# The recurrence's h held on chip by channel, and the chosen tokens' columns copied at register offsets

## The chip, the core and the metric

One core of a Trainium2 chip runs the whole kernel in one launch. The metric is the device time of one execution in microseconds, the median of several runs. The engines that work here are PE (TensorE, matmuls and transposes), DVE (VectorE), ACT (ScalarE), POOL (GpSimd) and SP (SyncE, which only issues DMAs). ACT and POOL issue some DMAs too.

## What is computed

```python
# x, f_logit: (4, 5056, 256); lower_bound: (256,)
f = lower_bound + (1 - lower_bound) * sigmoid(f_logit)
for t in range(5056):                  # for each of 4 batches and 256 channels
    h = f[:, t] * h + (1 - f[:, t]) * x[:, t]
    y[:, t] = h
tokens = y.reshape(20224, 256)
logits = tokens @ w_gate               # 8 experts
expert, gate = argmax(logits), softmax(logits) at the argmax
out = zeros(20224, 256)
for e in range(8):
    tok = the at most 80 tokens of expert e with the largest gate
    out[tok] = gate[tok] * (relu(tokens[tok] @ w1[e]) @ w2[e])   # w1 (8,256,1024), w2 (8,1024,256)
```

All is float32. At most 640 of the 20224 rows of the result are not zero.

## The kernel before, in words

The work has three stages.

**Stage 1, recurrence and logits (lines 105 to 283).** The sequence is cut into 10 groups of 512 tokens (the last one overlaps the one ahead of it), times 4 batches: 40 units of 512 tokens by 256 channels, run as a software pipeline in which each turn n of the loop at L271 does one step for several units. `load` (L126) brings f_logit and x of a unit, 512 KB each, token by partition. `gate` (L135, ACT) makes s, the complement of the sigmoid; `enter` (L139, POOL) makes u = s * x. `to_channels` (L143, PE) transposes both so that channels lie on the partitions: 8 transposes into `sp`, 8 into `up`, each half a unit in one PSUM bank, two buffers each. `decay` (L152, ACT) makes the factor a from sp, and `scan` (L159, DVE) runs the recurrence along the free axis into a tile `h`, from the last column of the same batch one group earlier. h is then used twice. `to_tokens` (L167) transposes it back: 8 transposes into the one PSUM buffer `hp` in two halves, the first copied out by ACT and the second by DVE into `ht`, which SP writes to `h_dram` (512 KB a unit). `logits` (L192, PE) multiplies h by the gate weights. After every fourth unit (a group) `by_token` transposes the logits and `choice` (DVE) finds each token's expert. After 5 groups, and after the last, `gates` computes the gate values and `candidates` puts them into `cand`, a table of 128 rows (expert, batch, token modulo 4) by 1264.

**Stage 2, selection (L306 to L374).** The weights of all 8 experts (2 MB each) and the zeros for the whole result (20.7 MB) are issued on SP's queue ahead of it, in the order at L298 to L304. `largest` (L315, DVE) takes the 80 largest of each row of `cand` in 10 rounds; they go through DRAM (`val_dram`, `id_dram`, issued by ACT) into 8 rows of 1280, and `largest` runs again. From the places found, 8 indirect DMAs (POOL, L362) fetch the token numbers of each expert's 80 slots, and 8 more (L368) fetch the tokens' rows of h from `h_dram`, 80 by 256.

**Stage 3, experts (L376 to L411).** `hidden(e)` transposes the rows (2 PE transposes), scales them (`xt`, DVE), and does 32 matmuls (order counts 16, each issued as two) with w1 and a ReLU (ACT). `result(e)` does the matmuls with w2, scales by the gate value (`y`, DVE) and scatters 80 rows (POOL). `hidden(e + 1)` stands ahead of `result(e)`.

The order of each engine's instructions is the order in which the program is written (`tc.manual_schedule`); waits between engines are semaphores that the tile layer puts in. An engine runs its own instructions in order.

Of the kernel before, what the change touches and what calls it, by code (L numbers as in the profile page):

```python
# [16 lines left out]
P = 128  # L17
# [5 lines left out]
def kernel(  # L23
# [46 lines left out]
    h_dram = dram.tile([N, D], F32, name="h_dram")  # L70
# [29 lines left out]
    shift = consts.tile([P, n_grp, C, E], F32, name="shift")  # L100
    chosen = consts.tile([P, n_grp, C, E], F32, name="chosen")
    nc.gpsimd.memset(shift, 0.0)
    ctx.enter_context(tc.manual_schedule())

    with tc.tile_pool(name="ld", bufs=5) as ld, \
         tc.tile_pool(name="sup", bufs=3) as sup, \
         tc.tile_pool(name="apool", bufs=2) as apool, \
         tc.tile_pool(name="hpool", bufs=B + 4) as hpool, \
         tc.tile_pool(name="htok", bufs=3) as htok, \
         tc.tile_pool(name="gsm", bufs=2) as gsm, \  # L110
         tc.tile_pool(name="psu", bufs=2, space=PSUM) as psu, \
         tc.tile_pool(name="ptp", bufs=1, space=PSUM) as ptp, \
         tc.tile_pool(name="plg", bufs=1, space=PSUM) as plg:

        xs, fs, sts, uts, sps, ups, decays, hs, lgs, lts, gms = ({} for _ in range(11))

        def setup():
            nc.vector.tensor_scalar(omlb, lb, -1.0, 1.0, ALU.mult, ALU.add)
            nc.vector.tensor_scalar(nomlb, lb, 1.0, -1.0, ALU.mult, ALU.add)
            for o in range(DC):  # L120
                nc.vector.tensor_scalar_mul(wg[:, o], wg[:, o], omlb[:, ds(o, 1)])
            bp = plg.tile([P, 1], F32, name="bp", tag="ct")
            nc.tensor.transpose(bp, base_row, ident[:1, :1])
            nc.vector.tensor_copy(base, bp)
# [10 lines left out]
        def gate(n):  # L135
            sts[n] = sup.tile([P, R, D], F32, name="s_t", tag="s_t")
            nc.scalar.activation(sts[n], fs.pop(n), ACT.Sigmoid, scale=-1.0)  # L137

        def enter(n):  # L139
            uts[n] = sup.tile([P, R, D], F32, name="u_t", tag="u_t")  # L140
            nc.gpsimd.tensor_tensor(uts[n], sts[n], xs.pop(n), ALU.mult)  # L141

        def to_channels(n, src, dst, tag):  # L143
            for o in range(DC):
                ps = psu.tile([P, G], F32, name=tag, tag=tag)
# [6 lines left out]
        def decay(n):  # L152
            for o in range(DC):
                a = apool.tile([P, G], F32, name="a", tag=f"a{o}")
                nc.scalar.activation(a, sps.pop((n, o)), ACT.Identity,  # L155
                                     scale=nomlb[:, ds(o, 1)], bias=1.0)
                decays[n, o] = a

        def scan(n):  # L159
            hs[n] = hpool.tile([P, DC, G], F32, name="h", tag="h")  # L160
            for o in range(DC):
                nc.vector.tensor_tensor_scan(  # L162
                    hs[n][:, o], decays.pop((n, o)), ups.pop((n, o)),
                    hs[n - B][:, o, ds(used(n // B - 1) - 1, 1)] if n >= B else 0.0,
                    ALU.mult, ALU.add)

        def to_tokens(n):  # L167
            g, b = divmod(n, B)
            ht = htok.tile([P, R, D], F32, name="ht", tag="ht")
            half = R // 2  # L170
            for i in range(2):
                hp = ptp.tile([P, half, D], F32, name="hp", tag="hp")
                for r in range(half):
                    for o in range(DC):
                        nc.tensor.transpose(hp[:, r, ds(o * P, P)],  # L175
                                            hs[n][:, o, ds((i * half + r) * P, P)], ident)
                copy = nc.scalar.copy if i == 0 else nc.vector.tensor_copy
                copy(ht[:, ds(i * half, half)], hp)  # L178
            lap = G - used(g)
            skip = lap if g == n_grp - 2 else 0  # L180
            out_t = h_dram[ds(b * S + first(g), G)].rearrange("(r p) d -> p r d", p=P)
            if skip:
                whole = (G - skip) // P
                nc.sync.dma_start(out=out_t[:, :whole], in_=ht[:, :whole])
                part = G - skip - whole * P
                if part:
                    nc.sync.dma_start(out=out_t[:part, whole], in_=ht[:part, whole])
            else:
                nc.sync.dma_start(out=out_t, in_=ht)


        def logits(n):  # L192
# [3 lines left out]
            hv = hs[n].rearrange("c o (p r) -> c o p r", r=R)  # L196
# [14 lines left out]
        def choice(g):  # L211
# [4 lines left out]
            def small(shape, name):  # L216
# [4 lines left out]
            sh = shift[:n_p, g]  # L221
# [5 lines left out]
            rv = small([C], "rv")  # L227
            nc.vector.tensor_reduce(rv, eq, AX.X, ALU.max)
            nc.vector.tensor_tensor(chosen[:n_p, g], eq,
                                    rv.unsqueeze(2).broadcast_to(full), ALU.is_equal)  # L230


        def gates(g0, g1):
            n = g1 - g0
            sh = shift[:, ds(g0, n)]
# [6 lines left out]
            for g in range(g0, g1):  # L242
                n_p = rows(g)
                gm = gsm.tile([P, E, C], F32, name="gm", tag="gm")[:n_p]
                nc.vector.tensor_tensor(
                    gm.rearrange("p e c -> p c e"), chosen[:n_p, g],
                    gt[:n_p, g - g0].unsqueeze(2).broadcast_to([n_p, C, E]), ALU.mult)
# [21 lines left out]
        AHEAD = 4  # L269
# [173 lines left out]
```

## Time and profile before

| | us |
|---|---|
| median of 3 runs | 488.58 (488.48 to 489.03) |
| the profiled execution, its own time | 486.84 |
| its span, first to last instruction | 485.1 |
| PE busy | 270.0 (56%) |
| DVE busy | 251.3 (52%) |
| ACT busy | 131.7 (27%) |
| POOL busy | 123.3 (25%) |
| moved by DMA | 101.93 MB |

The busy shares are means over three stages that have little in common, so they say little. Slices of the span show it: PE works in the first 58% and in the last 17% of the span and stands still between, while DVE is nearly full there. So the page is read stage by stage: which engine has work all the time, what the others wait for, and what the waiting costs in that stretch.

### The profile page before, as it was taken

The numbers are of one execution on the slowest core, as the hardware profiler recorded it, in microseconds if no ns is written. First come the engines' busy times: TensorE is split into PE (matmuls) and PEld (weight loads), VectorE is DVE, ScalarE is ACT, GpSimd is POOL, SyncE is SP. The second block draws the span as 40 slices with busy tenths as digits, with TensorE's granted clock in tenths as the row PEclk, the third lists the DMA queues.
The fourth block names the chain that finished last, engine by engine and source line by source line (L and its number), as shares of the span: only waits on it lengthen the run. The fifth ranks groups of instructions, "written<-read, shape, count | busy, mean of one in ns | idle before, by whom it ended". The sixth has DMA issues, their size and how long they took to land. (4 is left out here: it accounts for less than half of the span.)

```text
span 485.1 us, 5330 instructions
## 1 busy us (share of the span) xinstructions
PE 270.0 (56%) x2053; PEld 198.1 (41%) x2053; DVE 251.3 (52%) x335; ACT 131.7 (27%) x192; POOL 123.3 (25%) x77
## 2 busy tenths in 40 slices
PE   4886768768686486867687720000000003998985
PEld 3654545545554254545464410000000003977773
DVE  1555564555654755555644569995299951001010
ACT  4643443535254343435444120000000000101110
POOL 5543333414331132423331011000000037101011
PEclk9999897989798598989979865555555555599999
DMA  8988695969586456877852219999999501000000
GB/s 278 340 288 265 204 292 168 287 186 293 171 274 210 130 181 211 269 252 224 280 171 86 88 53 371 427 432 433 420 402 400 208 0 35 20 7 15 7 15 14
DMA packets 77001, 101.93 MB, mean 210 GB/s; under 512 B 3752, under 2 KB 73384, under 8 KB 75696
## 3 DMA queue, kind: packets, MB, share of 16 engines
q1 hardware_dynamic: 75104, 100.15, 59.5%
q0 software_dynamic: 1024, 1.31, 1.0%
q8 instruction: 16, 0.26, 0.2%
q10 hardware_dynamic: 848, 0.13, 0.2%
q14 instruction: 9, 0.07, 0.0%
HBM read 59.43 MB, written 42.16 MB: 209 GB/s over the span
## 5 line engine op out<-in xcount | busy, mean ns | idle before, releaser
L141 POOL TENSOR_TENSOR u_t<-s_t,x_t 128x1024 f32<-128x1024 f32 x40 | 94.7, 2368 | 162.4 <-ACT s_t L137 157.4
L162 DVE TENSOR_TENSOR_SCAN h<-a,h,up 128x512 f32<-128x512 f32 x72 | 87.9, 1263 | 0.0
L178 DVE COPY ht<-hp 128x512 f32<-128x512 f32 x40 | 27.7, 692 | 107.4 <-PE hp L175 107.4
L147 PE MATMUL up<-ident,u_t 128*128 128x128 f32 x320 | 56.6, 307 | 40.3 <-DVE h L162 39.0
L175 PE MATMUL hp<-ident,h 128*128 128x128 f32 x320 | 57.0, 306 | 27.1 <-ACT ht L178 27.1
L155 ACT ACTIVATE a<-sp,nomlb 128x512 f32<-128x512 f32 x80 | 51.1, 684 | 63.0 <-PE sp L147 61.5
L147 PEld LDWEIGHTS up<-ident,u_t 128*128 128x128 f32 x320 | 38.3, 154 | 57.2 <-issue 32.0
L348 PE MATMUL slots<-ident,at2f 8*80 8x8 f32 x1 | 0.2, 228 | 104.8 <-DVE at2f L344 104.8
L393 ACT ACTIVATE hid<-h_ps 128x480 f32<-128x480 f32 (+1 forms) x16 | 7.0, 438 | 184.7 <-PE h_ps L390 184.7
L175 PEld LDWEIGHTS hp<-ident,h 128*128 128x128 f32 x320 | 40.3, 155 | 38.6 <-ACT ht L178 37.8
L147 PE MATMUL sp<-ident,s_t 128*128 128x128 f32 x320 | 47.6, 297 | 4.2 <-ACT s_t L137 4.2
L178 ACT COPY ht<-hp 128x512 f32<-128x512 f32 x40 | 23.5, 586 | 85.5 <-PE hp L175 85.5
L147 PEld LDWEIGHTS sp<-ident,s_t 128*128 128x128 f32 x320 | 38.9, 152 | 15.9 <-issue 11.6
L199 PE MATMUL lg<-h,wg 128*32 128x128 f32 x640 | 44.1, 406 | 0.0
L137 ACT ACTIVATE s_t<-f_t 128x1024 f32<-128x1024 f32 x40 | 42.5, 1063 | 4.5 <-DMA f_t<-in_f_logit_dram 4.5
L348 PEld LDWEIGHTS slots<-ident,at2f 8*80 8x80 f32 x1 | 0.1, 138 | 105.1 <-DVE at2f L344 105.1
L390 PE MATMUL h_ps<-xt,w_sb 128*128 128x80 f32 x256 | 36.8, 313 | 5.0 <-issue 4.1
L390 PEld LDWEIGHTS h_ps<-xt,w_sb 128*128 128x128 f32 x256 | 35.7, 227 | 6.2 <-issue 4.9
L318 DVE MAX8 val<-cand 128x8 f32<-128x1264 f32 (+1 forms) x20 | 29.6, 1480 | 14.3 <-DMA cand<-val_dram 13.7
L402 DVE TENSOR_SCALAR y<-y_ps,gsl 80x256 f32<-80x256 f32 x8 | 3.8, 480 | 58.1 <-PE y_ps L399 58.1
L399 PE MATMUL y_ps<-w_sb,hid 128*80 128x256 f32 x128 | 30.6, 396 | 0.0
L319 DVE FIND_INDEX8 at<-val,cand 128x8 uint32<-128x1264 f32 (+1 forms) x20 | 29.4, 1470 | 0.0
(58 smaller groups left out, 181.1 us busy)
## 6 DMA issues: line engine op xcount, KB each, us to landing
f_t<-in_f_logit_dram SPq DMA_DIRECT2D x40, 512.0 KB, 5.0
x_t<-in_x_dram SPq DMA_DIRECT2D x40, 512.0 KB, 5.6
h_dram<-ht SPq DMA_DIRECT2D x36, 512.0 KB, 3.3
out_dram<-zero SPq DMA_DIRECT2D x9, 2048.0 KB, 24.3
w_sb<-in_moe_w_dram SPq DMA_DIRECT2D x16, 1024.0 KB, 11.6
out_dram<-zero SPq DMA_DIRECT2D x1, 1792.0 KB, 24.5
h_dram<-ht SPq DMA_DIRECT2D x4, 384.0 KB, 2.5
h_dram<-ht SPq DMA_DIRECT2D x4, 64.0 KB, 2.2
```

Source lines behind the costliest of these rows:

```text
L137: nc.scalar.activation(sts[n], fs.pop(n), ACT.Sigmoid, scale=-1.0)
L141: nc.gpsimd.tensor_tensor(uts[n], sts[n], xs.pop(n), ALU.mult)
L147: nc.tensor.transpose(ps[:, ds(r * P, P)], src[n][:, r, ds(o * P, P)], ident)
L155: nc.scalar.activation(a, sps.pop((n, o)), ACT.Identity, scale=nomlb[:, ds(o, 1)], bias=1.0)
L162: nc.vector.tensor_tensor_scan(hs[n][:, o], decays.pop((n, o)), ups.pop((n, o)), hs[n - B][:, o, ds(used(n // B - 1) - 1, 1)] if n >= B el ...
L175: nc.tensor.transpose(hp[:, r, ds(o * P, P)], hs[n][:, o, ds((i * half + r) * P, P)], ident)
L178: copy(ht[:, ds(i * half, half)], hp)
L199: nc.tensor.matmul(lgs[g][ds(r * LC, LC), b], wg[:, o], hv[:, o, :, r], start=o == 0, stop=o == DC - 1, skip_group_check=True)
L318: nc.vector.max(out=top, in_=src)
L319: nc.vector.max_index(out=at[:, ds(k, TOP)], in_max=top, in_values=src)
L390: nc.tensor.matmul(h_ps[:, c], w1_sb[e][:, o, ds((c0 + c) * P, P)], xt[:, o], start=o == 0, stop=o == DC - 1, skip_group_check=True)
L399: nc.tensor.matmul(y_ps, hid[:, c], w2_sb[e][:, c], start=c == 0, stop=c == FC - 1)
```

## The change

h is no longer written to DRAM. One tile `h_all` holds it for all 20224 tokens, channel by partition (128 partitions of 2 x 20224 floats, 158 KB each). `decay` writes the factor straight into h's place, and `scan` runs in place there. `to_tokens`, the `ht` copies and the writes to `h_dram` are gone. To make room, `gate` and `enter` work in place in the loaded tiles (4 buffers of each, where there were 5 and 3 of the products), and loads are issued 3 turns ahead where it was 4; `up` has 4 PSUM buffers where it had 2. `chosen` is not stored: `choice` keeps only the winning code (`pick`), and `gates` makes the one-hot table again, one DVE instruction more for each group.

Only expert 0's weights are loaded ahead of the selection; the zeros follow in 40 writes of at most 512 KB. After the token numbers have come (one tile `tok` of 80 by 8 now), they are cast, transposed to `trow` (8 rows of 80) and loaded into registers, 16 at a time. For each of the 640 slots one engine then copies one column of `h_all` (128 partitions, 2 elements) into `xe`, at the offset in the register. Runs of 16 slots go to DVE, ACT, POOL, DVE, ACT for each expert. Then `h_all` is released, and the weights of experts 1 to 7 are loaded into its room. `hidden` scales `xe` with no transpose.

The core of the diff (the parts left out are names and pools):

```diff
-    h_dram = dram.tile([N, D], F32, name="h_dram")
...
+    h_all = hpool.tile([P, DC, N], F32, name="h_all")
...
         def gate(n):
-            sts[n] = sup.tile([P, R, D], F32, name="s_t", tag="s_t")
-            nc.scalar.activation(sts[n], fs.pop(n), ACT.Sigmoid, scale=-1.0)
+            sts[n] = fs.pop(n)
+            nc.scalar.activation(sts[n], sts[n], ACT.Sigmoid, scale=-1.0)
...
         def decay(n):
             for o in range(DC):
-                a = apool.tile([P, G], F32, name="a", tag=f"a{o}")
-                nc.scalar.activation(a, sps.pop((n, o)), ACT.Identity,
+                nc.scalar.activation(h_all[:, o, ds(spot(n), G)], sps.pop((n, o)), ACT.Identity,
                                      scale=nomlb[:, ds(o, 1)], bias=1.0)
...
+                h = h_all[:, o, ds(spot(n), G)]
                 nc.vector.tensor_tensor_scan(
...
+                    h, h, ups.pop((n, o)),
+                    h_all[:, o, ds(spot(n) - 1, 1)] if n >= B else 0.0, ALU.mult, ALU.add)
-        def to_tokens(n):
...
-                nc.sync.dma_start(out=out_t, in_=ht)
...
+                nc.vector.tensor_tensor(oh, revexp[:n_p].unsqueeze(1).broadcast_to(full),
+                                        pick[:n_p, g].unsqueeze(2).broadcast_to(full),
+                                        ALU.is_equal)
...
-        AHEAD = 4
+        AHEAD = 3
...
-            unit(to_tokens, n - 1)
...
+    EARLY = 1
...
+    for e in range(EARLY):
+        weights(wpool, e)
...
+    ZR = 4
...
-            nc.gpsimd.indirect_dma_start(
-                out=xe, out_offset=None, in_=h_dram,
-                in_offset=bass.IndirectOffsetOnAxis(ap=toks[e], axis=0))
...
+        rp = psl.tile([E, K], F32, name="rp")
+        nc.tensor.transpose(rp, tokf, ident[:K, :K])
+        trow = xpool.tile([E, K], I32, name="trow")
+        nc.vector.tensor_copy(trow, rp)
...
+        SHARE = 16
+        X = []
+        for e in range(E):
+            xe = xpool.tile([P, DC, K], F32, name=f"xe{e}")
+            for i, k in enumerate(range(0, K, SHARE)):
+                engine, copy = ways[i % len(ways)]
+                n = min(SHARE, K - k)
+                _, at_tok = nc.values_load_multi_w_load_instructions(
+                    trow[ds(e, 1), ds(k, n)], engines=(engine,), min_val=0, max_val=N - 1,
+                    skip_runtime_bounds_check_because="token numbers come from iota")
+                for j, v in enumerate(at_tok):
+                    copy(xe[:, :, ds(k + j, 1)], h_all[:, :, ds(v, 1)])
+            X.append(xe)
+        hpool.release()
+        wlate = ctx.enter_context(tc.tile_pool(name="wlate", bufs=1, side="right"))
+        for e in range(EARLY, E):
+            weights(wlate, e)
...
-            for o in range(DC):
-                nc.tensor.transpose(xt_ps[:, o], X[e][:, ds(o * P, P)], ident[:K, :K])
...
-                nc.vector.tensor_scalar_mul(xt[:, o], xt_ps[:, o], omlb[:, ds(o, 1)])
+                nc.vector.tensor_scalar_mul(xt[:, o], X[e][:, o], omlb[:, ds(o, 1)])
```

PE in stage 1, before, around the end of a group (`sp` and `up` are the transposes of s and u, `hp` those of h, `lg` the logits, `lt` their transposes):

```order
L147 MATMUL sp<-ident,s_t 128x128 x8
L147 MATMUL up<-ident,u_t 128x128 x8
L175 MATMUL hp<-ident,h 128x128 x8
L199 MATMUL lg<-h,wg 32x128 x8
L207 MATMUL lt<-ident,ls 128x128 x4
```

The same place with the change:

```order
L152 MATMUL sp<-ident,f_t 128x128 x8
L152 MATMUL up<-ident,x_t 128x128 x8
L177 MATMUL lg<-h_all,wg 32x128 x8
L185 MATMUL lt<-ident,ls 128x128 x4
L152 MATMUL sp<-ident,f_t 128x128 x8
```

The eight `hp` transposes between `up` and `lg` are gone; nothing else moved on PE.

DVE between selection and experts, with the change (`goal` is the row to scatter to, `trow` the token numbers by expert; ISA is a register instruction that works out the copy's address from a token number):

```order
L352 TENSOR_TENSOR goal_2034<-tok,far 80x1
L359 CAST trow<-rp 8x80
L371 TENSOR_LOAD trow
L375 ISA
L375 COPY xe_2040<-h_all 128x2
```

The last two rows stand there 16 times behind each of 16 such loads, 256 copies in all; ACT has the same 16 and 256, POOL 8 and 128. Before, DVE went from the eighth `goal` straight to the `xt` scaling.

SP, before, behind the last write of h (the two DMAs of expert 1 and those of experts 2 to 7 follow in the same form):

```order
L189 DMA h_dram<-ht 128x4x256 x4
L295 DMA w_sb_2640<-in_moe_w_dram 128x2x1024
L296 DMA w_sb_2648<-in_moe_w_dram 128x8x256
L295 DMA w_sb_2641<-in_moe_w_dram 128x2x1024
L296 DMA w_sb_2649<-in_moe_w_dram 128x8x256
L302 DMA out_dram<-zero 128x4096 x9
```

SP with the change, behind the last load of x:

```order
L274 DMA w_sb_1863<-in_moe_w_dram 128x2x1024
L276 DMA w_sb_1865<-in_moe_w_dram 128x8x256
L290 DMA out_dram<-zero 128x1024 x39
L290 DMA out_dram<-zero 128x512
L274 DMA w_sb_4012<-in_moe_w_dram 128x2x1024
```

Of the weights only expert 0's stand ahead of the zeros; the row that starts with w_sb_4012 (expert 1) waits for the last copy on DVE, ACT and POOL.

## Rows read from the trace of the kernel before

**Rows 1.** Busy time by stretch: us, PE, PEld, DVE, ACT, POOL busy (instructions), PEclk, DMA share, GB/s.
```profile
4.00:15.00 11.00, 7.61 (x40) 7.06 (x40) 4.14 (x8) 6.94 (x9) 7.14 (x3) 1.00 1.08 376
...
289.46:394.71 105.25, 0.30 (x2) 0.21 (x2) 89.12 (x101) 0.00 (x0) 3.92 (x3) 0.50 0.89 358
...
408.25:485.10 76.85, 67.30 (x398) 56.70 (x398) 7.01 (x23) 7.00 (x16) 11.89 (x13) 0.88 0.06 16
```
**Rows 2.** Waits between 20 and 260 us: total us, times, longest.
```profile
PE up L147 <- DVE h L162: 35.5, 37, 2.8
...
PE hp L175 <- ACT ht L178: 23.7, 35, 0.7
```
**Rows 3.** Timeline of a unit in stage 1: start us, us, instruction [idle before].
```profile
103.89 2.37 POOL L141 TENSOR_TENSOR u_t<-s_t,x_t 128x1024 f32<-128x1024 f32 x1 [6.84 <-ACT s_t L137]
...
109.07 1.10 PE L199 MATMUL lg<-h,wg 128*32 128x128 f32 x16
...
109.47 2.37 POOL L141 TENSOR_TENSOR u_t<-s_t,x_t 128x1024 f32<-128x1024 f32 x1 [3.20 <-ACT s_t L137]
109.79 2.44 DVE L162 TENSOR_TENSOR_SCAN h<-a,h,up 128x512 f32<-128x512 f32 x2
...
110.10 1.09 PE L147 MATMUL sp<-ident,s_t 128*128 128x128 f32 x8
...
110.79 1.26 ACT L155 ACTIVATE a<-sp,nomlb 128x512 f32<-128x512 f32 x2 [1.40 <-PE sp L147]
...
111.20 0.63 PE L147 MATMUL up<-ident,u_t 128*128 128x128 f32 x4
```
**Rows 4.** Timeline, the first unit's transposes of u.
```profile
9.36 1.97 PE L147 MATMUL up<-ident,u_t 128*128 128x128 f32 x8 [1.12 <-POOL u_t L141]
```
**Rows 5.** Timeline of POOL around the gate values of the first five groups.
```profile
160.58 2.34 POOL L141 TENSOR_TENSOR u_t<-s_t,x_t 128x1024 f32<-128x1024 f32 x1 [10.30 <-ACT s_t L137]
172.91 2.37 POOL L141 TENSOR_TENSOR u_t<-s_t,x_t 128x1024 f32<-128x1024 f32 x1 [9.99 <-ACT s_t L137]
```
**Rows 6.** Timeline, end of stage 1.
```profile
268.61 0.66 PE L147 MATMUL up<-ident,u_t 128*128 128x128 f32 x4 [0.45 <-DVE h L162]
...
280.16 0.29 DVE L220 TENSOR_REDUCE mx<-lt 128x16 f32<-128x128 f32 x1 [1.71 <-PE lt L207]
...
289.46 1.48 DVE L318 MAX8 val<-cand 128x8 f32<-128x1264 f32 x1
```
**Rows 7.** Groups by line and form: xcount | busy us, mean ns | idle before.
```profile
L318 DVE MAX8 val<-cand 8x8 f32<-8x1280 f32 x10 | 14.8, 1482 | 14.0 <-DMA cand<-val_dram 13.7
...
L393 ACT ACTIVATE hid<-h_ps 128x480 f32<-128x480 f32 x8 | 4.6, 571 | 180.9 <-PE h_ps L390 180.9
...
L393 ACT ACTIVATE hid<-h_ps 128x160 f32<-128x160 f32 x8 | 2.4, 304 | 3.8 <-PE h_ps L390 3.8
```
**Rows 8.** DMA issues: count, KB each, us to landing.
```profile
tok<-id_dram,place POOLq DMA_INDIRECT x8, 2.2
...
val_dram<-val ACTq DMA_DIRECT2D x1, 40.0 KB, 9.3
```
**Rows 9.** Timeline from the selection to the first expert.
```profile
394.25 0.16 DVE L351 CAST place<-slots 80x8 int32<-80x8 f32 x1 [0.39 <-PE slots L349]
394.33 0.15 DVE L353 COPY gsl<-slots 80x8 f32<-80x8 f32 x1
...
403.40 0.91 POOL L362 DMA_INDIRECT tok<-id_dram,place  x1 [0.30 <-issue]
...
408.26 7.12 PE L390 MATMUL h_ps<-xt,w_sb 128*128 128x80 f32 x32 [0.40 <-DVE xt L382]
```
**Rows 10.** Instructions of L403: count, duration ns min/median/max, first and last start.
```profile
L403 POOLq MOVE  x8: 29/29/29, 405.8 to 477.2; - x8
```
**Rows 11.** Timeline between two experts in stage 3.
```profile
436.44 0.48 DVE L402 TENSOR_SCALAR y<-y_ps,gsl 80x256 f32<-80x256 f32 x1 [7.16 <-PE y_ps L399]
436.84 0.50 DVE L382 TENSOR_SCALAR xt<-xt_ps,omlb 128x80 f32<-128x80 f32 x2
...
437.23 2.99 PE L390 MATMUL h_ps<-xt,w_sb 128*128 128x80 f32 x25 [0.69 <-issue]
```

More of the change, by code (lines that the diff above doesn't have):

```diff
@@ L99, with spot @@
     BATCHES = 2
-    shift = consts.tile([P, n_grp, C, E], F32, name="shift")
-    chosen = consts.tile([P, n_grp, C, E], F32, name="chosen")
+    per_batch = -(-n_grp // BATCHES)
+    shift = consts.tile([P, per_batch, C, E], F32, name="shift")
     nc.gpsimd.memset(shift, 0.0)
+    pick = consts.tile([P, n_grp, C], F32, name="pick")
+    hpool = tc.alloc_tile_pool(name="hpool", bufs=1, side="right")
+    h_all = hpool.tile([P, DC, N], F32, name="h_all")
     ctx.enter_context(tc.manual_schedule())
[L105 to L112, printed above, removed]
+    with tc.tile_pool(name="ld", bufs=4) as ld, \
+         tc.tile_pool(name="gsm", bufs=1) as gsm, \
+         tc.tile_pool(name="pss", bufs=2, space=PSUM) as pss, \
+         tc.tile_pool(name="psu", bufs=4, space=PSUM) as psu, \
          tc.tile_pool(name="plg", bufs=1, space=PSUM) as plg:
-        xs, fs, sts, uts, sps, ups, decays, hs, lgs, lts, gms = ({} for _ in range(11))
+        xs, fs, sts, uts, sps, ups, lgs, lts, gms = ({} for _ in range(9))
+        def spot(n):
+            g, b = divmod(n, B)
+            return b * S + first(g)
         def setup():
@@ L226, in choice @@
                 op0=ALU.is_ge, op1=ALU.mult)
[L227 to L230, printed above, removed]
+            nc.vector.tensor_reduce(pick[:n_p, g], eq, AX.X, ALU.max)
         def gates(g0, g1):
             n = g1 - g0
-            sh = shift[:, ds(g0, n)]
+            sh = shift[:, ds(0, n)]
             nc.scalar.activation(sh, sh, ACT.Exp)
@@ L268, with begin @@
         batches = {g: (ends[i - 1] + 1 if i else 0, g + 1) for i, g in enumerate(ends)}
-        AHEAD = 4
+        AHEAD = 3
+        def begin(g):
+            return next(g0 for g0, g1 in batches.values() if g0 <= g < g1)
         setup()
@@ L302 @@
         nc.sync.dma_start(out=out_z[:, ds(k * D, n)], in_=zero[:, :n])
-    for e in range(2, E):
-        load_weights(e)
     with tc.tile_pool(name="sel", bufs=1) as sel, \
-         tc.tile_pool(name="xp", bufs=E) as xp, \
-         tc.tile_pool(name="mp", bufs=2) as mp, \
          tc.tile_pool(name="psl", bufs=1, space=PSUM) as psl, \
-         tc.tile_pool(name="psx", bufs=2, space=PSUM) as psx, \
          tc.tile_pool(name="psh", bufs=2, space=PSUM) as psh, \
@@ L366 @@
+        nc.vector.tensor_copy(tokf, tok)
+        goals = []
         for e in range(E):
-            xe = xp.tile([K, D], F32, name="xe", tag="xe")
-            nc.gpsimd.indirect_dma_start(
-                out=xe, out_offset=None, in_=h_dram,
-                in_offset=bass.IndirectOffsetOnAxis(ap=toks[e], axis=0))
-            X.append(xe)
-            goal = sel.tile([K, 1], I32, name=f"goal{e}")
-            nc.vector.tensor_tensor(goal, toks[e], far[:, ds(e, 1)], ALU.add)
-            goals.append(goal)
+            goal = sel.tile([K, 1], I32, name=f"goal{e}")
+            nc.vector.tensor_tensor(goal, tok[:, ds(e, 1)], far[:, ds(e, 1)], ALU.add)
+            goals.append(goal)
@@ new lines @@
+        rp = psl.tile([E, K], F32, name="rp")
+        nc.tensor.transpose(rp, tokf, ident[:K, :K])
+        trow = xpool.tile([E, K], I32, name="trow")
+        nc.vector.tensor_copy(trow, rp)
+        ways = [(mybir.EngineType.DVE, nc.vector.tensor_copy),
+                (mybir.EngineType.Activation, nc.scalar.copy),
+                (mybir.EngineType.Pool, nc.gpsimd.tensor_copy)]
+        SHARE = 16
[10 more added lines that the diff above has]
+                    copy(xe[:, :, ds(k + j, 1)], h_all[:, :, ds(v, 1)])
+            X.append(xe)
@@ L376, in hidden @@
+        hpool.release()
+        wlate = ctx.enter_context(tc.tile_pool(name="wlate", bufs=1, side="right"))
+        for e in range(EARLY, E):
+            weights(wlate, e)
+        mp = ctx.enter_context(tc.tile_pool(name="mp", bufs=2, side="right"))
         def hidden(e):
[L377 to L379 removed]
             xt = mp.tile([P, DC, K], F32, name="xt", tag="xt")
```

80 lines of the change are left out of this document (27 added, 53 removed).

## The prediction, made before the changed kernel had run

> **What bounds the kernel now.** I read the stretches first, then the waits inside the longest one, then one unit of it, then the two seams. The stretches [rows 1] show three stages: up to 289.5 us the recurrence, then 105 us in which DVE has 89 us of work and PE none, then 77 us in which PE has 67. The change touches the first stage, the seam between the second and the third, and what DMA moves meanwhile. In the first stage no engine is full. PE waits 35.5 us for scans to free an `up` buffer and 23.7 us for ACT to empty the one `hp` buffer [rows 2]. One unit shows the same [rows 3]: `u_t` starts every 5.58 us (103.89 and 109.47), while in it PE's own work without `hp` is short: 1.10 us from the start of the 8 `sp` transposes to the start of `up`, as much again for `up`, and 1.03 us for the logits (109.07 to 110.10), 3.23 us in all. DVE's two scans take 2.44 us, POOL 2.37, ACT's two factors 1.26. So a unit is 5.58 us long because of a loop (PE to ACT to PE through `hp`, PE to DVE to PE through `up`), and the end of each group adds to it: the wait ahead of `u_t` is 6.84 us there and 3.20 otherwise.
>
> **Stage 1.** Removed: 320 `hp` transposes, 80 copies, 40 writes of 512 KB. With them goes the first loop. The second has twice the buffers. What is late next? PE at 3.23 us a unit plus a quarter of the group's `lt` transposes, say 3.33; DMA, which with loads alone moved 376 GB/s at a full share in the first 15 us [rows 1], so 1.05 MB of a unit in 2.8 us; then DVE with 2.44 and its choice operations, POOL with 2.37. All are below the 5.58 of today, and PE is the longest. The loop through the load buffers is no longer than that: from the end of `up` in a buffer to the next `up` in it there are an issue, a landing and POOL's 2.37 us, for four units. I take 3.6 us a unit, the PE figure and a little for the engines missing each other. The bounds are 3.3 (PE alone) and the 5.58 of today. From the first unit's `up`, which ends at 11.3 us [rows 4] as before, 39 units at 3.6 give 140.4: 151.7 us. The gate values of the first five groups hold PE up in the middle: the two waits there are 10.30 and 9.99 us [rows 5] where a group's seam and a usual turn have 6.84 and 3.20 [rows 3], 10.2 us more. I keep that whole, 162 us; the five one-hot tables made again go into it. At the end the last `up` is at 269.3 us now and the first operation on the last logits at 280.2, 10.9 us [rows 6], most of it three units' `hp` work in turn; scan, logits, copy and transposes alone I put at 5.5. From there to the selection it is 9.3 us, plus five one-hot operations at 0.29 us (the price of `mx`), 10.7. So the selection starts at 178 us, not at 289.5: **minus 111 us**.
>
> **Selection.** Its DVE work is unchanged. Its one wait is 13.7 us for the 40 KB that go through DRAM [rows 7], of which 9.3 are the landing of `val` behind the zeros [rows 8]. The zeros now start with the last `up`, 16 us ahead of the selection, behind one expert's weights and not two: 22.8 MB at 358 GB/s and a share of 0.89 [rows 1], so 402 at a full share, take 57 us and end about 41 us into the selection. `val` leaves after 29 operations of 1.48 us [rows 6], 43 us into it. Two hops of the 2.2 us that a small transfer takes [rows 8] and their issues make 5 us: **minus 8.7**. If I am wrong about the queue, nothing is gained there; nothing is lost either, since the last zeros wait for `val`.
>
> **The seam, and the copies.** Token numbers come as before, the last issued at 403.4 us [rows 9], landed at 405.6. Now all eight must be there: cast, eight `goal` operations, a transpose and the cast to `trow`, 1.4 us. Then the copies, C; then the scaling, 0.6; the first expert's matmuls stood at 408.26 [rows 9], so **minus 0.7 plus C**. Nothing covers C: DVE scales expert 0's columns only behind its own 256 copies, so PE waits for all of them.
>
> C is the one term that the trace does not show. DVE and ACT carry 256 copies each, with a register instruction ahead of each and 16 loads of 16 registers; POOL has half. *Per copy:* the lower bound is 0.08 us, the distance of two small DVE operations (394.25 and 394.33 [rows 9]). For ACT the ReLUs of 480 and of 160 elements take 571 and 304 ns [rows 7], 0.83 ns an element, so 0.17 us without any element. The upper bound is that plus the 0.30 us that POOL's issue leaves between two DMAs at register-like work [rows 9], 0.47. A register move on POOL takes 29 ns [rows 10], far nearer to nothing than to 0.30, so address work should run ahead of the engine; I take 0.17 on ACT, the slower of the two: 256 x 0.17 = 43.5 us. *Per load of 16 registers:* the lower bound is 16 moves of 29 ns, 0.46 us; the upper 16 times 0.30, 4.8 us. It is a round trip to memory for a few words, so I take the row that is nearest to that, the 2.2 us of `tok` [rows 8]: 16 x 2.2 = 35 us. **C = 79 us**, between 28 (0.08 and 0.46) and 197 (0.47 and 4.8).
>
> The ReLUs read PSUM; the copies read SBUF, for which no row of ACT is small enough. [...]
>
> **Weights.** 14.7 MB wait for the last copy and then take 36 us at 402 GB/s. Expert 1's first MB is there after 2.6 us and a 2.2 us trip, 4.8 us; PE needs it after expert 0's 7.12 us [rows 9]. Each further expert needs 5.2 us of DMA and eight take PE 77 us [rows 1], so I cost this at nothing; its cover is PE's own work, and at half the rate the last experts would wait some 10 us. The transposes of `xe` go, but PE still stands between experts until DVE has done `y` and `xt` behind it (436.44 to 437.23 [rows 11]): nothing gained.
>
> **Sum.** 485.1 - 111 - 8.7 - 0.7 + 79 = 443.7 us of span. The profiled execution took 486.84, 1.7 more than its span, and the median of the runs, 488.58, is 1.7 more again: **447 us**, 41 less than now.
>
> **Rivals.**
> *Cheap columns.* Register work is hidden and loads are fast: C = 28, 396 us. For it: the 29 ns move; against it: no load of many values is that quick in this trace.
> *Loads register by register.* Each register is a trip of its own, at the 0.30 us of POOL's issue 4.8 us a load: C = 43.5 + 77 = 120, 488 us, no change. Against it: one instruction loads sixteen. [...]
> *Dear copies, slower than now.* The engine stands while its own register instruction and the copy's address are worked out, 0.47 us a copy: C = 120 + 35 = 155, 523 us. It decides from the point where C eats the rest of the gain, 121 us: 0.33 us a copy with my price of a load. For it: a copy of two elements has nothing behind which to hide its address, and it follows its register instruction at once. Against it: the 29 ns.
> *Stage 1 stays bound by its seams.* With PE fuller, DVE's choice operations and POOL meet more often, or DVE's in-order scans hold PE as today, 4.5 us a unit: plus 35, 482 us; from 4.7 on it is slower than now. For it: 35.5 us of waits for scans today; against: twice the buffers, and DVE has 3 us of work a unit at most.
> That the change does not do what it says I see no room for: the order of instructions has no wait between the copies.
>
> **Numbers.** Forecast 0.55 (418 to 478: C of 55 to 105, a unit of 3.4 to 3.9). Cheap columns 0.15, loads register by register 0.10, dear copies 0.08, seams 0.12. A measurement of this kernel tells changes of over 0.2%, 1 us, from none. Slower are the dear copies, and of the register loads and the seams a third each: 0.15. Within 0.2% I put 0.02, faster 0.83. The range that leaves out the lower half of the cheap case (0.07), the dear copies and a part of the two others (0.13 together) is 400 to 488.
>
> **What would show it.** Right: `u_t` starts 3.4 to 3.9 us apart; the first MAX8 at 165 to 190 us with PE nearly full before it; the wait for `cand` near 5 us; then a stretch of 55 to 105 us with 256 tiny copies on ACT as the last to end, PE still; then experts as before with no wait for weights. Wrong: units above 4.5 us; copies over 0.3 us apart; a load that takes 3 us or more, or under 1; PE waiting for `w_sb`.

## The result and the profile after

The changed kernel takes **407.64 us** (median of 4 runs, 407.11 to 408.09) where the kernel before took 488.53 in the same comparison (4 runs, 488.42 to 489.03): a ratio of 0.834, 95% interval 0.833 to 0.836, 81 us less. The prediction said 447 and 400 to 488. The direction was right and the time lies in the range, but the gain is twice the forecast: 407.6 is below the 418 to 478 of the forecast case, and the range held it because it took in half of the cheap case. The profiled execution has a span of 405.3 us.

Stretches of the changed kernel, with the columns of [rows 1]: its first 11 us, the early and the late part of stage 1, the selection, and the experts.
```profile
4.00:15.00 11.00, 7.48 (x34) 7.08 (x35) 3.89 (x8) 6.29 (x8) 6.75 (x3) 1.00 1.10 349
20.00:84.00 64.00, 58.73 (x624) 42.90 (x616) 52.76 (x54) 44.40 (x62) 46.19 (x20) 1.00 1.03 328
108.00:150.00 42.00, 39.53 (x420) 29.20 (x412) 35.09 (x38) 29.54 (x43) 30.26 (x13) 1.00 0.85 278
171.80:268.50 96.70, 0.27 (x2) 0.20 (x2) 89.13 (x101) 0.00 (x0) 0.58 (x2) 0.50 0.43 174
331.01:405.30 74.29, 64.95 (x384) 54.16 (x384) 6.33 (x23) 7.00 (x16) 7.36 (x8) 0.89 0.59 207
```
In stage 1 PE is busy 92 and 94% of the time, and DMA has a share of 1.03 in the first of the two stretches: two resources are full at once, where none was (PE 74% and DMA 0.78 between 20 and 84 us before). The selection lost 8.6 us against [rows 1]. Between 268.5 and 331.0 lies a new stage, the copies.

Waits between 20 and 160 us of the changed kernel: total us, times, longest.
```profile
POOL x_t L146 <- ACT f_t L142: 41.2, 29, 10.1
DVE mx L198 <- PE lt L185: 19.9, 9, 4.3
PE ct L234 <- DVE gm L225: 10.1, 5, 6.2
...
PE up L152 <- DVE h_all L165: 2.8, 8, 0.6
```
PE's wait for scans, 35.5 us between 20 and 260 us before [rows 2], is 2.8 here, and those for `hp` are gone. What is left for PE is mostly the middle, where the gate values of five groups are made.

Groups of the changed kernel by line and form: count | busy us, mean ns | idle us before, and what ended it.
```profile
L301 DVE MAX8 val<-cand 8x8 f32<-8x1280 f32 x10 | 14.8, 1482 | 5.4 <-DMA cand<-val_dram 5.1
...
L375 DVE COPY xe<-h_all 128x2 f32 x256 | 30.5, 179 | 19.6 <-issue 19.6
L375 ACT COPY xe<-h_all 128x2 f32 x256 | 26.2, 190 | 134.2 <-issue 134.2
...
L394 PE MATMUL h_ps<-xt,w_sb 128*128 128x80 f32 x256 | 36.6, 313 | 55.6 <-DVE xt L386 50.9 <-issue 4.7
```
The wait for `cand`, 13.7 us in [rows 7], is 5.1. The last line is the price of the change in one number: PE stands 50.9 us for the columns once it has transposed the token numbers. From the cast of the places to the first expert it is 63.0 us now (268.04 to 331.01), where it was 14.0 (394.25 to 408.26 [rows 9]).

Two lines of the changed kernel, 371 (the loads of registers) and 375 (a register instruction and a copy), by instruction: count, duration in ns (min/median/max), first and last start in us.
```profile
L371 ACTq TENSOR_LOAD <-trow x16: 1017/1024/1219, 280.5 to 319.9; - x16
L371 DVEq TENSOR_LOAD <-trow x16: 1097/1100/1345, 280.6 to 327.4; - x16
...
L375 DVEq FUSED_REGOPS  x256: 46/46/46, 282.0 to 330.3; - x128
L375 DVE COPY xe<-h_all x256: 154/170/258, 282.1 to 330.4; 128x2 f32 x128
```
Timelines of DVE in the changed kernel at the start of the copies and at their end, and of ACT's first turn: start us, us, instruction [idle before].
```profile
282.13 1.91 DVE L375 COPY xe<-h_all 128x2 f32 x16 [1.68 <-issue]
285.15 1.89 DVE L375 COPY xe<-h_all 128x2 f32 x16 [1.10 <-issue]
288.15 1.67 DVE L375 COPY xe<-h_all 128x2 f32 x14 [1.12 <-issue]
290.12 0.28 DVE L375 COPY xe<-h_all 128x2 f32 x2 [0.30 <-issue]
...
328.67 1.89 DVE L375 COPY xe<-h_all 128x2 f32 x16 [1.12 <-issue]
```
```profile
281.90 1.61 ACT L375 COPY xe<-h_all 128x2 f32 x16 [119.32 <-issue]
```
On DVE a turn of 16 columns is a load of 1.1 us, then 16 copies 0.118 us apart (1.89 / 16), 3.0 us in all. The last copy of DVE ends at 330.6, of ACT at 322.9, of POOL, with half as many, at 305. DVE is the engine that the experts wait for.

### The profile page after: what moved, and what is told of

It reads as the page before. It is cut to its first block, busy times and chain, and to the rows that moved or that the text cites. A ratio compares the mean times of both kernels' runs of the same rounds, so it can differ in the third digit from the quotient of the medians.

```text
span 405.3 us, 5826 instructions
## 1 busy us (share of the span) xinstructions
PE 200.4 (49%) x1718; PEld 153.0 (38%) x1718; DVE 255.1 (63%) x553; ACT 134.2 (33%) x408; POOL 129.5 (32%) x197
## 5 line engine op out<-in xcount | busy, mean ns | idle before, releaser
L146 POOL TENSOR_TENSOR x_t<-f_t,x_t 128x1024 f32<-128x1024 f32 x40 | 94.8, 2369 | 53.3 <-ACT f_t L142 41.2
L165 DVE TENSOR_TENSOR_SCAN h_all<-h_all,up 128x512 f32<-128x512 f32 x80 | 95.1, 1253 | 6.9 <-PE up L152 5.7
L159 ACT ACTIVATE h_all<-sp,nomlb 128x512 f32<-128x512 f32 x80 | 50.9, 684 | 44.0 <-PE sp L152 44.0
L394 PE MATMUL h_ps<-xt,w_sb 128*128 128x80 f32 x256 | 36.6, 313 | 55.6 <-DVE xt L386 50.9
L152 PE MATMUL sp<-ident,f_t 128*128 128x128 f32 x320 | 45.9, 290 | 4.2 <-ACT f_t L142 4.2
L152 PE MATMUL up<-ident,x_t 128*128 128x128 f32 x320 | 45.5, 284 | 5.0 <-DVE h_all L165 2.8
L177 PE MATMUL lg<-h_all,wg 128*32 128x128 f32 x640 | 44.2, 404 | 6.4 <-ACT ls L182 4.8
L142 ACT ACTIVATE f_t<-f_t 128x1024 f32<-128x1024 f32 x40 | 42.4, 1061 | 9.7 <-DMA f_t<-in_f_logit_dram 9.7
L152 PEld LDWEIGHTS sp<-ident,f_t 128*128 128x128 f32 x320 | 37.6, 148 | 16.0 <-ACT f_t L142 10.8
L375 DVE COPY xe<-h_all 128x2 f32 x256 | 30.5, 179 | 19.6 <-issue 19.6
L152 PEld LDWEIGHTS up<-ident,x_t 128*128 128x128 f32 x320 | 38.2, 147 | 7.5 <-DVE h_all L165 3.9
L331 PEld LDWEIGHTS slots<-ident,at2f 8*80 8x80 f32 x1 | 0.1, 135 | 96.7 <-issue 96.7
L403 PE MATMUL y_ps<-w_sb,hid 128*80 128x256 f32 x128 | 29.6, 386 | 0.0
```

Source lines behind the costliest of these rows:

```text
L142: nc.scalar.activation(sts[n], sts[n], ACT.Sigmoid, scale=-1.0)
L146: nc.gpsimd.tensor_tensor(uts[n], sts[n], uts[n], ALU.mult)
L152: nc.tensor.transpose(ps[:, ds(r * P, P)], src[n][:, r, ds(o * P, P)], ident)
L159: nc.scalar.activation(h_all[:, o, ds(spot(n), G)], sps.pop((n, o)), ACT.Identity, scale=nomlb[:, ds(o, 1)], bias=1.0)
L165: nc.vector.tensor_tensor_scan(h, h, ups.pop((n, o)), h_all[:, o, ds(spot(n) - 1, 1)] if n >= B else 0.0, ALU.mult, ALU.add)
L177: nc.tensor.matmul(lgs[g][ds(r * LC, LC), b], wg[:, o], hv[:, o, :, r], start=o == 0, stop=o == DC - 1, skip_group_check=True)
```

## The experiments

Each was timed beside the kernel before; ratios are to that, with their 95% intervals. Four ask what the copies' stage is made of, five what stage 1 is made of, and three put the way back to tokens somewhere else.

**What a column costs.** Two kernels take parts of it away, one changes the size of a load, one the split over engines.

Constant columns, no loads and no register instructions:
```
-                _, at_tok = nc.values_load_multi_w_load_instructions(...)
+                at_tok = [(e * K + k + j) * 31 + 5 for j in range(n)]
```


> The changed kernel with the 640 copies at offsets that are constants in the program, so without the 40 register loads and the register instruction ahead of each copy (the columns copied are then not the chosen tokens'). In the changed kernel the copy phase is 50 us on DVE: 16 loads of 1.10 us and 256 copies 0.118 us apart. Theory (a load stands in the engine's own order and nothing runs meanwhile, and a copy's distance is that of the copy itself): the loads go, 17.6 us, the distance stays 0.118, the phase is 31 us and the time 388 us. Rival (the register instruction sets the distance between copies): the distance falls to the 0.08 us of two plain small DVE operations too, the phase is 20 us and the time 378 us. Second rival (loads run ahead while copies drain): the phase hardly changes, 405 us.

Measured: 377.96 us, ratio 0.776 (0.774 to 0.779), the rival's value. Timeline of DVE in this kernel:
```profile
280.76 19.64 DVE L373 COPY xe<-h_all 128x2 f32<-128x2 f32 x256
```
and its line 373 on ACT, by instruction (columns as for line 375 above):
```profile
L373 ACT COPY xe<-h_all x256: 188/188/195, 219.2 to 243.3; 128x2 f32<-128x2 f32 x128
```
Without a register instruction ahead of it, a copy of DVE follows the last after 0.077 us, not 0.118. The 0.041 us between the two is nearly the 46 ns that a `FUSED_REGOPS`, the register instruction, takes on DVE: most of it is not hidden behind the copies. The edit also frees the other engines' copies from the token numbers: ACT makes its 256 in the selection, POOL starts at 278.3. That is not what shortens DVE's distance, since in the changed kernel DVE's last turn (328.67), when ACT and POOL have ended, takes 1.89 us like the others. On ACT the register instruction costs nothing: its copies follow each other after 0.095 us here (24.1 us from the first start to the 256th) and in the changed kernel alike (16 in 1.61 us, of which the last one lasts 0.19).

One copy of 80 neighbouring columns per expert:
```
-            for i, k in enumerate(range(0, K, SHARE)):
...
+            nc.vector.tensor_copy(xe, h_all[:, :, ds(e * 2000, K)])
```


> The changed kernel with one copy of 80 neighbouring columns for each expert on DVE in place of 80 copies at register offsets (so the tokens are not the chosen ones); all waits around them stay. Theory: the whole phase of 50 us is the loads and copies themselves, so about 48 us go and the time is 359 us, with the first expert's matmuls some 3 us after the token numbers are on chip. Rival: a part of the 50 us is a wait for something else (the release of the memory, a queue), and the time stays above 370 us. If the late weights were hidden only by luck, PE would now wait for them in the same way as in the changed kernel, since they still start when the copies end.

Measured: 359.17 us, ratio 0.738 (0.736 to 0.740). Timeline of PE in this kernel:
```profile
282.36 13.94 PE L387 MATMUL h_ps<-xt,w_sb 128*128 128x80 f32 x64 [1.91 <-DVE xt L379]
```
Its first `h_ps` starts at 282.36, and no matmul waits for weights, so their late loading is hidden with the whole of the copies' stage taken away too.

`SHARE = 8`, twice the loads at half the registers:

> The changed kernel with 8 registers to a load where it has 16: DVE again has 256 copies, behind 32 loads; ACT and POOL have 192 each. It tells what a load's 1.10 us is made of. If each register is a trip of its own, a load of 8 is 0.55 us, DVE's phase stays 48 to 50 us and the time 408 us. If a load has a fixed price, it stays 1.10 us, the phase is 256 x 0.118 + 32 x 1.10 = 65 us and the time 423 us. Between the two the length of a load gives both parts.

Measured: 410.4 us, ratio 0.843 (0.841 to 0.845), the theory's 408 more than the rival's 423. Line 371 of this kernel:
```profile
L371 DVEq TENSOR_LOAD <-trow x32: 595/597/835, 280.7 to 331.6; - x32
```
16 registers take 1.100 us, 8 take 0.597: 0.063 us a register and 0.09 us for the load itself. (DVE carries 32 loads of 8 here, 256 columns as before.)

The turn of the engines goes on from expert to expert, so that the 40 turns split 14, 13, 13 and not 16, 16, 8:
```
-                engine, copy = ways[i % len(ways)]
+                engine, copy = ways[(i + e * (K // SHARE)) % len(ways)]
```


> The changed kernel with the runs of 16 slots dealt in turn over DVE, ACT and POOL through all 40 runs (14, 13 and 13 of them) where each expert starts again with DVE (16, 16 and 8). Theory (the phase is as long as the engine with the most work, and the engines do not slow each other): DVE has 14 runs of 3.1 us, 44 us where it has 50, POOL 13 of 3.04, 40 us; the time is 401 to 402 us, ratio to before 0.821. Rival (POOL and DVE share the way to the memory, and more copies on POOL slow DVE's): the distance of DVE's copies rises over 0.118 us, and the gain is under 3 us.

Measured: 401.74 us, ratio 0.825 (0.823 to 0.826). The first `h_ps` moves from 331.01 to 324.98: two turns of DVE at 3.0 us. POOL's extra copies, 16 in 2.06 us, do not slow DVE's, which still take 1.89.

**Where stage 1's 118 us came from.** The first `MAX8` of the selection marks the end of stage 1: 289.46 us before, 171.82 after (timeline of DVE in the changed kernel):
```profile
171.82 1.48 DVE L301 MAX8 val<-cand 128x8 f32<-128x1264 f32 x1 [0.18 <-DMA out_dram<-zero]
```

The kernel before without the way back:
```
-            unit(to_tokens, n - 1)
...
-                out=xe, out_offset=None, in_=h_dram,
+                out=xe, out_offset=None, in_=x.rearrange("b s d -> (b s) d"),
```


> The kernel before without the way back to tokens (no hp, no ht, no h_dram); the selected rows are gathered from x in place of h, so the values differ and the rest of the work stays. Theory (the way back, by its PE, ACT, DVE and DMA work and by what it made x_t and f_t wait for, was what stage 1 paid for; in-place h and four up buffers add little): a unit comes to some 3.9 us with the waits at the groups, the first MAX8 is issued near 187, and the whole takes 385 to 388 us, ratio 0.79. Rival (most of the gain comes from the four up buffers and from the scan in place): MAX8 not before 220, the whole over 420 us, ratio over 0.86.

Measured: 394.69 us, ratio 0.810 (0.806 to 0.814); timeline of DVE in this kernel:
```profile
198.55 1.48 DVE L317 MAX8 val<-cand 128x8 f32<-128x1264 f32 x1
```
That is nearer to the theory than to the rival, but 11 us later than the theory said, and that four `up` buffers add little does not hold: the next two runs show it.

The changed kernel with two and with three `up` buffers (`psu`, `bufs=4` to 2, to 3):

> The changed kernel with two PSUM buffers for up in place of four. Theory (the deeper up buffers let PE run ahead of the scan, and with them PE is busy 92% of stage 1; two would bring back part of PE's wait for the scans): 10 to 15 us slower than the changed kernel, 418 to 422 us, ratio 0.855 to 0.865. Rival (PE's wait for the scans in the kernel before was only the scans' wait for the way back): no change, 406 to 409 us, ratio 0.834.

> The changed kernel with three PSUM buffers for up. With two, POOL's steps show one of 7 to 8.7 us in every group of four, with four buffers none. Theory (what the buffers hide is DVE's work of a group, some 4 us each time, and each buffer hides half a unit of it): about half of the 28 us comes back, 419 to 425 us, ratio 0.86 to 0.872. Rival (it takes a whole unit of buffers, since a unit uses two): three are as good as two, 433 to 437 us, ratio 0.895.

Measured: 435.48 us with two, ratio 0.895 (0.890 to 0.901), `MAX8` at 199.71; 427.2 us with three, ratio 0.875 (0.872 to 0.879), `MAX8` at 190.46. So two buffers cost 28 us, about twice what I had expected, and the third gives back 9, the fourth 19; three buffers lie between theory and rival. PE's wait for the scans between 20 and 160 us, with two buffers:
```profile
PE up L152 <- DVE h_all L165: 22.0, 14, 3.4
```
Timeline of POOL through a group of four units, first with two buffers:
```profile
52.67 2.35 POOL L146 TENSOR_TENSOR x_t<-f_t,x_t 128x1024 f32<-128x1024 f32 x1 [1.11 <-ACT f_t L142]
59.94 2.37 POOL L146 TENSOR_TENSOR x_t<-f_t,x_t 128x1024 f32<-128x1024 f32 x1 [4.92 <-ACT f_t L142]
62.86 2.37 POOL L146 TENSOR_TENSOR x_t<-f_t,x_t 128x1024 f32<-128x1024 f32 x1 [0.55 <-ACT f_t L142]
66.59 2.35 POOL L146 TENSOR_TENSOR x_t<-f_t,x_t 128x1024 f32<-128x1024 f32 x1 [1.36 <-ACT f_t L142]
70.05 2.35 POOL L146 TENSOR_TENSOR x_t<-f_t,x_t 128x1024 f32<-128x1024 f32 x1 [1.11 <-ACT f_t L142]
```
and in the changed kernel, with four:
```profile
45.53 2.36 POOL L146 TENSOR_TENSOR x_t<-f_t,x_t 128x1024 f32<-128x1024 f32 x1 [1.04 <-ACT f_t L142]
48.99 2.37 POOL L146 TENSOR_TENSOR x_t<-f_t,x_t 128x1024 f32<-128x1024 f32 x1 [1.10 <-ACT f_t L142]
51.91 2.39 POOL L146 TENSOR_TENSOR x_t<-f_t,x_t 128x1024 f32<-128x1024 f32 x1 [0.56 <-ACT f_t L142]
55.38 2.36 POOL L146 TENSOR_TENSOR x_t<-f_t,x_t 128x1024 f32<-128x1024 f32 x1 [1.07 <-ACT f_t L142]
58.79 2.37 POOL L146 TENSOR_TENSOR x_t<-f_t,x_t 128x1024 f32<-128x1024 f32 x1 [1.05 <-ACT f_t L142]
```
Both have steps of 2.9 to 3.7 us inside a group. With two buffers one step in four is 7.3 us (52.67 to 59.94), and four take 17.4; with four buffers no step stands out, and four take 13.3.

The kernel before with three `up` buffers (`ct` and `bp` take the buffer of `lt`, as in the changed kernel, which frees a PSUM buffer):
```
-            ct = plg.tile([P, P], F32, name="ct", tag="ct")
+            ct = plg.tile([P, P], F32, name="ct", tag="lt")
...
-         tc.tile_pool(name="psu", bufs=2, space=PSUM) as psu, \
+         tc.tile_pool(name="pss", bufs=2, space=PSUM) as pss, \
+         tc.tile_pool(name="psu", bufs=3, space=PSUM) as psu, \
```


> The kernel before with three PSUM buffers for up (ct takes the buffer of lt, as in the changed kernel, which frees the bank; a fourth has no room). Its steps in a group of four are 5.6, 5.6, 6.1 and 9.2 us. Theory (the buffers pay only where PE is the limit; before, DVE's copies of ht and the wait for hp set the unit): 480 to 489 us, ratio 0.985 to 1.0. Rival (the long step in each group, some 3.5 us eight times, is the same stall as in the changed kernel with two buffers): 465 to 478 us, ratio 0.955 to 0.98.

Measured: 452.24 us, ratio 0.926 (0.923 to 0.929), `MAX8` at 254.10. Neither expectation covers it: one PSUM buffer more gives the kernel before 37 us. POOL in this kernel, from one group's end through the next:
```profile
46.28 2.37 POOL L142 TENSOR_TENSOR u_t<-s_t,x_t 128x1024 f32<-128x1024 f32 x1 [5.67 <-ACT s_t L138]
52.41 2.38 POOL L142 TENSOR_TENSOR u_t<-s_t,x_t 128x1024 f32<-128x1024 f32 x1 [3.76 <-ACT s_t L138]
57.11 2.37 POOL L142 TENSOR_TENSOR u_t<-s_t,x_t 128x1024 f32<-128x1024 f32 x1 [2.32 <-ACT s_t L138]
62.29 2.37 POOL L142 TENSOR_TENSOR u_t<-s_t,x_t 128x1024 f32<-128x1024 f32 x1 [2.81 <-ACT s_t L138]
70.32 2.38 POOL L142 TENSOR_TENSOR u_t<-s_t,x_t 128x1024 f32<-128x1024 f32 x1 [5.66 <-ACT s_t L138]
```
PE's wait for the scans between 20 and 160 us, in the kernel before and then in this one:
```profile
PE up L147 <- DVE h L162: 22.1, 23, 2.8
```
```profile
PE up L148 <- DVE h L163: 11.5, 5, 2.3
```
The wait of 3.20 us in an ordinary unit of the kernel before [rows 3] is 2.32 here, and the step 4.70 us in place of 5.58. PE's wait for scans (37 times in [rows 2]) was thus a loop of every unit, not an affair of the group's end: with the third buffer it comes 5 times where it came 23 times. The `hp` buffer did not set the unit by itself, as I had assumed for the expectation.

Half of the logits matmuls left out:
```
-            for o in range(DC):
+            for o in range(1):
                 for r in range(R):
...
-                                     start=o == 0, stop=o == DC - 1, skip_group_check=True)
+                                     start=o == 0, stop=o == 0, skip_group_check=True)
```


> The changed kernel with the logits of the first 128 channels alone: 4 of the 8 logits matmuls of each unit are left out, so other tokens are chosen. About 0.5 us of PE work per unit goes. If PE alone bounds stage 1 now, 40 units give 20 us: 387 us, ratio 0.795. If the loads (1 MB per unit, DMA share 1.0) or DVE stand right behind PE, 5 to 12 us: 396 to 403 us, ratio 0.81 to 0.825. If the loads bound it already, no change: 406 to 409 us, ratio 0.834.

Measured: 399.39 us, ratio 0.820 (0.816 to 0.824); `MAX8` at 163.05, so 8.8 us of PE's 20 come back. Of three candidates it is the middle one: PE sets the unit, with others right behind. Timeline of POOL in this kernel:
```profile
48.04 2.36 POOL L146 TENSOR_TENSOR x_t<-f_t,x_t 128x1024 f32<-128x1024 f32 x1 [0.63 <-ACT f_t L142]
50.65 2.37 POOL L146 TENSOR_TENSOR x_t<-f_t,x_t 128x1024 f32<-128x1024 f32 x1 [0.24 <-DMA x_t<-in_x_dram]
```
It waits for loads of `x_t` in places now, and the steps are some 3 us, the pace of the loads: between 20 and 84 us DMA moves 343 GB/s in this kernel, at a share of 1.07, and 1.05 MB a unit at that rate is 3.1 us.

**The way back, put where PE and ACT are idle.** In the selection PE has 0.27 us of work in 96.7. Three kernels keep stage 1 of the changed kernel, transpose `h_all` to tokens during the selection, store it, and gather rows as the kernel before does. ACT issues those stores, so `val`, the ids and `cand` go through SP's queue in its place:
```
+        for n in range(n_unit):
+            ht = htok.tile([P, R, D], F32, name="ht", tag="ht")
+            for i in range(2):
+                hp = ptp.tile([P, half, D], F32, name="hp", tag="hp")
...
+                nc.scalar.copy(ht[:, ds(i * half, half)], hp)
...
+            nc.scalar.dma_start(out=out_t, in_=ht)
+    hpool.release()
```


> The changed kernel with stage 1 as it is, but with the way back to tokens put into the selection, where PE and ACT have nothing to do: 320 transposes from h_all, 80 PSUM copies on ACT, 40 stores to h_dram, then the gather by rows and the transposes of the kernel before in place of the copies at register offsets. Theory (the selection is DVE's alone and hides that work; the seam falls back from 62.5 to some 14 us): first MAX8 at 172, slots near 270, first h_ps near 285, the whole 358 to 366 us, ratio 0.735 to 0.75. Rival (the selection cannot hide it: at PE's lower clock 320 transposes take some 2.1 us per unit, 84 us, and the zeros and the rows together are 41 MB, 98 us at the 420 GB/s that the zeros reached, so slots or the gather wait): the whole 375 to 395 us, ratio 0.77 to 0.81.

Measured: 389.71 us, ratio 0.799 (0.795 to 0.804): faster than the changed kernel, but the rival's value. Timeline of DVE in this kernel:
```profile
247.85 1.48 DVE L332 MAX8 val<-cand 8x8 f32<-8x1280 f32 x1 [30.92 <-DMA cand<-val_dram]
```
In SP's queue `val` and `cand` stand behind 40 stores of zeros, while the rows are stored too: DMA's share is 1.04 between 172 and 200 us and 1.02 between 200 and 230. So the stores of zeros were split, 8 ahead of `val` and 32 behind `cand`:
```
-        nc.sync.dma_start(out=out_z[:, ds(k * D, n)], in_=zero[:, :n])
+    zeros(0, 32)
...
+        zeros(32, N // P)
```


> As e_late_back, but 8 of the 40 stores of zeros are issued at the start of the selection and 32 after cand2 has been asked for, in place of all 40 at the start. In e_late_back DVE stood 30.9 us for cand2, since val and cand2 went through the queue behind the zeros, and ACT stood 45.7 us for the stores of rows. Theory (the order in one queue was the cost, not the work): the wait for cand2 falls to 5 to 8 us, slots come near 272 to 276, the first h_ps near 287 to 292, and the whole takes 362 to 370 us, ratio 0.745 to 0.76. Rival (the transfers themselves are too many, 41 MB beside 16 MB of weights): the zeros move behind the gather and delay it or the late weights, and the whole stays at 380 to 390 us.

Measured: **373.93 us**, ratio 0.766 (0.763 to 0.768), the fastest kernel here that leaves nothing out. The wait for `cand` is 4.5 us, as the theory said; the total is 4 to 12 us over it. Timeline of PE in this kernel:
```profile
259.08 1.97 PE L305 MATMUL hp<-ident,h_all 128*128 128x128 f32 x8 [25.82 <-ACT ht L308]
...
278.41 0.23 PE L366 MATMUL slots<-ident,at2f 8*80 8x8 f32 x1 [0.82 <-ACT ht L308]
...
295.36 0.53 PE L399 MATMUL xt_ps<-ident,xe 80*128 80x80 f32 x2 [16.65 <-DMA xe<-h_dram,tok]
```
and the group of ACT, which copies `hp` and issues the rows, between 165 and 320 us:
```profile
L308 ACT COPY ht<-hp 128x512 f32<-128x512 f32 x80 | 43.2, 589 | 72.1 <-DMA out_dram<-zero 26.7 <-PE hp L305 24.0 <-DMA h_dram<-ht 14.6
```
The last rows meet the zeros: DMA's share is 1.03 between 230 and 260 us, ACT's waits whose end the trace puts down to a store of zeros come to 26.7 us, and `slots`, in PE's order behind them, comes 11 us after DVE's last operation on `at2f` (267.4). The third kernel lets ACT issue the 32 stores behind its last store of rows:

> As e_late_back2, but the 32 stores of zeros are issued by ACT behind its last store of rows. In e_late_back2 PE stood 25.8 us at 259.1 for a ht buffer whose store shared the engines with the zeros, slots came at 278.4 in place of some 268, and the first xt_ps at 295.4. Theory (that wait alone held slots back): no wait of that kind, slots at 267 to 270, first xt_ps at 280 to 286 (the indirect gathers still meet zeros and weights), the whole 358 to 367 us, ratio 0.735 to 0.75. Rival (the bytes have to go somewhere: 16 MB of zeros and 14 MB of late weights now meet the gather and the first experts): slots at 268 but PE waits for w_sb of expert 1 or the gather takes over 20 us, the whole 370 to 376 us, ratio 0.757 to 0.77.

Measured: 401.69 us, ratio 0.824 (0.819 to 0.829), outside both. Timelines of this kernel, of PE and then of ACT and its issues:
```profile
266.39 0.20 PE L366 MATMUL slots<-ident,at2f 8*80 8x8 f32 x1 [18.57 <-DVE at2f L362]
...
284.63 7.11 PE L410 MATMUL h_ps<-xt,w_sb 128*128 128x80 f32 x32 [0.39 <-DVE xt L402]
...
333.13 7.12 PE L410 MATMUL h_ps<-xt,w_sb 128*128 128x80 f32 x32 [41.12 <-ACT hid L413]
```
```profile
249.44 83.03 ACTq L291 DMA_DIRECT2D out_dram<-zero  x32
332.51 0.77 ACT L413 ACTIVATE hid<-h_ps 128x480 f32<-128x480 f32 x2 [83.52 <-DMA w_sb<-in_moe_w_dram]
```
The first half went as the theory said: `slots` at 266.4, the first `h_ps` at 284.6. But ACT was issuing stores until 332.5, 83 us for 32 of them (DMA's share is 1.04 between 260 and 300 us; why an issue took that long, no run shows), and the ReLU of expert 0 stood behind them in ACT's order; PE lost 41 us to that. The same stores from SP, which computes nothing, but gated on the last store of rows, were not tried.

## Why the prediction was right in direction and 40 us too high

**Stage 1, forecast −111, measured −117.6.** Right, and by the mechanism told. Four units take 13.26 us (45.53 to 58.79), 3.3 each, which was my lower bound for PE alone; I took 3.6, and 3.3 lies just under the 3.4 to 3.9 that I had named as the sign. The middle, which I kept whole at 10.2 us, is still there: POOL's waits ahead of 92.27 and 104.75 are 4.58 and 10.14 us. From PE's last `up`, which ends at 154.0, to `MAX8` it is 17.8 us; I had 16.2.

What I could not have read is how the parts share the gain, and they do not add. Removing the way back alone gives 90.9 us (289.46 to 198.55); keeping `h` in place gives nothing beside it (199.71 with two buffers); the third and fourth `up` buffer give the last 28. But one more buffer in the kernel before gives 35 with the way back in place. The rival of the seams, 4.5 us a unit where DVE's choice operations and in-order scans hold PE, is what happens with two buffers: 17.4 us for four units, 4.35 each. The four buffers keep it away: PE's wait for the scans between 20 and 160 us is 22.0 us with two and 2.8 with four. By the program a unit takes two buffers, so four let PE run a whole unit ahead while DVE works on a group. The prediction named the buffers in half a sentence; they carry a quarter of stage 1's gain.

**Selection, forecast −8.7, measured −8.6.** Right: the wait for `cand` fell to 5.1 us, since `val` lands in 1.5 us with DMA idle ahead of it (a share of 0.00 from 210 to 216 us).

**The seam and C, forecast −0.7 + 79, measured +49.** This is the step that failed: **C is 50 us, not 79**. The first `h_ps` is at 331.01, in the kernel with block copies at 282.36; with the 1.28 us of those eight copies the register copies cost 49.9. That is under the 55 to 105 of the forecast. Its two terms were both priced too high:

- *A load of 16 registers* I priced at 2.2 us, the landing of a small DMA. It takes 1.10 on DVE: 17.6 us for 16 where I had 35. The register-by-register rival (4.8 us a load) had the form right: half the registers take 54% of the time. Its price was wrong, 0.063 us a register and not 0.30. That a load is a round trip to memory, my reason for the 2.2, no run shows.
- *A copy* I priced at 0.17 us on ACT. One does last 0.190 there, but they overlap: 16 in 1.61 us, 0.10 apart. DVE's are 0.118 apart. 256 on DVE make 30.2 us where I had 43.5. The 30.2 are 19.6 of copies (the constant columns) and 10.6 that come with the register instructions, which I had hoped would run ahead of the engine; on ACT they do (0.095 us between copies with and without them), on DVE they do not (0.118 against 0.077).

17.6 and 30.2 are 47.8; the other 2 us are the start of the first load and short gaps, below. I also had the wrong engine as the last: DVE, not ACT, since ACT hides its register instructions (37 ns each) and DVE most of the 46 ns not, and since a load takes 1.100 us on DVE and 1.024 on ACT. The "cheap columns" and the "dear copies" both fell: 0.08 us a copy is reached only on DVE with no register instruction, 0.47 nowhere.

**Weights, forecast 0.** Right, and still so without the stage of copies ahead of them. The experts take 74.3 us where they took 76.9 [rows 1]: 2.6 less that I had put at nothing.

The errors: −6.6 in stage 1, −29 in C, −2.6 in the experts; with the small ones they make the 39 us between 447 and 407.6.

## What to carry to other kernels

Where one engine stands for another's buffer in every unit, try a buffer more before a redesign: the third `up` buffer was worth 37 us in the kernel before and 8 in the changed one (435.48 to 427.2), so measure it in the kernel that will have it. Before work is taken out of a full stage at the cost of a slow gather, look for a stage where the engines that do that work are idle: the kernel with the way back in the selection is 34 us faster than the one with the register copies that replaced it. And an engine that computes should not issue a long row of large stores while DMA is full (a share of 1.04): ACT was held 83 us by them, and PE 41 us behind ACT.

## What the runs showed of the hardware that I had not expected

- A copy of two elements on DVE, with constant addresses, follows the last after 0.077 us although one lasts 0.150; a register instruction ahead of each makes that 0.118. On ACT it is 0.095 with and without one.
- With constant addresses, beside DVE's copies at 0.077 us, POOL's 128 take 18.94 us, 0.148 each, where with registers, beside DVE's at 0.118, 16 take 2.0 to 2.1, some 0.13 each. Why, no run shows.
- The 16 copies of a turn are now and then cut in two by a gap of 0.16 to 0.30 us (the third turn shown: 14 copies, 0.30, 2 copies), again after 62 more copies, on all three engines. With loads of 8 registers (`SHARE = 8`) it comes after 60 on DVE. Both are about 128 instructions, loads and register instructions counted. DVE's row of 256 copies at constant addresses has no such gap. Why it comes, no run shows.
- ACT stood 83 us in issuing 32 stores of at most 512 KB, 16.5 MB in all, while DMA's share was 1.04 between 260 and 300 us.
